# Attention and two gated MLPs on one core: the first MLP's weights are put together in another way, and head splitting begins one pair sooner

## The chip, the cores and the metric

The kernel runs on one core of a Trainium2 chip. The metric is the device time of one execution in microseconds (us), the median over the runs; lower is better. The engines are PE (TensorE, matrix products; PEld is its loading of weights), DVE (VectorE), ACT (ScalarE), POOL (GpSimd) and SP (SyncE, which issues the DMAs).

## The reference

Three stages, in float32. Attention has 4 batches, 8 heads, 576 positions and 64 columns a head; scores further than `tau` below the maximum of their row are cut off:

```
scores = scale * q @ k.T
scores = where(scores >= max(scores) - tau, scores, -1e9)
attn = exp(scores - max(scores)); attn = attn / (sum(attn) + 1e-9)
x = (attn @ v) gathered to 2304 tokens x 512
h = x @ w_in;  x = (h * sigmoid(h)) @ w_out        # first MLP, 512 -> 2048 -> 512
y = ((x @ w_a) * (x @ w_b)) @ w_out2               # second MLP, 512 -> 1536 -> 512
```

The weights are float64. The kernel reads each as two 32-bit words and builds the float32 value by hand.

## The kernel before, in words

**Products in two halves.** A float32 value is kept as a high half (rounded to the matmul's `fp32r` format) and a low half (the rest). A product is then three `fp32r` matmuls: weight low by data high, weight high by data high, weight high by data low.

**Attention.** The 4 x 8 heads are taken in 16 pairs, of which batch 0 has its four in two halves each. The unit of work is a tile of up to 128 query rows, numbered 0 to 143 (`softmax`): scores on PE (L537 or L544), the row minimum of the negated scores on DVE (L555), a threshold on DVE (L564), the exponential on ACT (L570), the mask on DVE (L573), then transposes on PE (L612), their copies out of PSUM on ACT, and the product with v on PE (L690). A head below tile `SPLIT_FROM` is loaded plainly (`load_head`) and its scores are float32 matmuls over 64 rows (L544). From there on it is split into halves first (`split_head`: cast on ACT, L457; subtraction on DVE, L460; five pieces on POOL, L463) and its scores are `fp32r` matmuls over 128 rows (L537).

**First MLP.** `w_in` and `w_out` are cut into 32 tiles of 128 x 512 (`w1_chunk`, `split_weight`). For each, a DMA brings the raw 64-bit words; ACT casts the low words to small integers (L358) and scales the high words (L363); DVE takes the sign bit (L369), shifts the scaled word left by three and joins the sign (L374); the low word is added, in four pieces on POOL for tiles 0 to 15, on DVE for 16 to 31 (L379); ACT casts the high half (L383), DVE subtracts the low half (L387). The tokens are taken in seven blocks, each against 16 slices of the hidden width: products up (L813), tanh, gate and halves (L823 to L832), products down (L873). These units follow one another strictly in order, so block 1 begins behind block 0, which needs all 32 weight tiles.

**Second MLP.** Its weights are prepared during attention and the first MLP and parked in DRAM; its products (L1184, L1270) come last.

**What sets the order.** `Plan` is a list scheduler that runs when the program is built: each task has an engine, a cost in ns, a rank and its dependencies; whenever an engine is free, its ready task of lowest rank goes next. The result is a fixed order for each engine. Ranks of attention are the tile's number plus `SHIFT`; the weight tile `i` has rank `W_AT + W_STEP * i + W_SHIFT[i]`; MLP work has ranks of 1000 and up, so it fills what attention leaves. `RINGS` gives the number of buffers: a task that takes a buffer waits, in order, until the one so many before it is freed. The raw weight tiles lie in a pool that is closed behind the last of the 32 (`closed0`), and the split heads' tiles are put in its place, so `split_head`'s cast is behind `closed0`.

Of the kernel before, what the change touches and what calls it, by code (L numbers as in the profile page):

```python
# [11 lines left out]

F32 = mybir.dt.float32
F32R = mybir.dt.float32r
U32 = mybir.dt.uint32
AF = mybir.ActivationFunctionType
ALU = mybir.AluOpType
PSUM = bass.MemoryType.PSUM
# [3 lines left out]
P = 128  # L22
# [23 lines left out]
N_YW, N_SW, N_TW = 14, 12, 6  # L46
# [5 lines left out]


W_AT, W_STEP = 2, 1.3
SHIFT = {1: -0.8, 8: 1.8, 14: 0.3, 19: -0.3, 23: -0.6, 25: -1.7, 27: -1.3, 28: -0.2, 29: 0.7,
         30: -0.4, 33: 0.9, 36: 1.0, 54: 1.9, 55: -2.5, 64: -2.1, 65: -1.1, 74: 5.6, 88: -1.0,
         96: -2.5, 108: -1.2, 115: -2.5, 129: 1.7, 132: -2.9}
W_SHIFT = {1: -1.8, 2: 3.2, 3: 3.9, 4: 6.8, 5: 3.5, 6: 3.4, 7: 5.1, 8: 4.1, 9: 7.4, 10: 7.9, 11:
           7.9, 12: 7.9, 13: 7.9, 14: 6.5, 15: 11.2, 16: 8.0, 17: 4.1, 18: 8.0, 19: 3.6, 20: 5.2,
           21: 6.3, 22: 10.2, 23: 10.2, 24: 8.2, 25: 8.5, 26: 11.1, 27: 10.2, 28: 10.2, 29: 10.2,  # L60
           30: -0.6, 31: 11.0}

SLACK = 2000

R_T, R_AV, R_EV, R_NORM = 2, 3, 1, -2
R_LD, R_SPLIT, R_AUX, R_MLP = -9, -6, -1, 1000

SPLIT_FROM = 54

EARLY = 16  # L70
IN_PSUM = 0
# [10 lines left out]
PIECE = 128  # L82

LO_ON = ("DVE",)

SCALE_ON = ("ACT",)
# [130 lines left out]
def dve_ns(n, fast=False):  # L217
    return int(n / (1.92 if fast else 0.96) + 67)


def pool_ns(n):
    return int(2.5 * n + 95)


def pieces(n, most):

    k = -(-n // most)
    return [slice(n * i // k, n * (i + 1) // k) for i in range(k)]
# [7 lines left out]
def fused_kernel(ctx: ExitStack, tc: tile.TileContext, qk, qk2, v, tau, w_in, w_out, w_a, w_b, w_o2, out):  # L236
# [9 lines left out]
    nc = tc.nc  # L246
    pl = Plan()
# [10 lines left out]
    def pool(stack, name, bufs, side="left", **kw):  # L258
        return stack.enter_context(tc.tile_pool(name=name, bufs=bufs, side=side, reuse_waits="tile", **kw))

    const = pool(ctx, "const", 1)
    pools = {n: pool(ctx, n, size) for n, size in (("wy", N_YW), ("ws", N_SW), ("wz", N_TW))}
    p1, p1x, px, att, attp, psb = (ExitStack() for _ in range(6))
    RINGS = dict(qk0=1, qk1=1, sp=2, aw=1, v=1, t=2, e=2, tl=1, si=1, pa=1, pb=1, sa=1, sb=1, tp=2, hb=1, hc=1, yc=1, yd=1, ye=1, yf=1, xr5=3, x5=5, g5=2, th5=1, av=1, x=1, xi=1, rs=1,
                 xr=2, xb=6, g=2, th=1, yo=2, wraw=2, wc=1, wt=2, wy=N_YW, ws=N_SW, wz=N_TW,
                 ur=2, uw=3, vr=1, vw=2, yr=1, pr=4, tm=4, a11=2, zh=3, zl=2, **{f"z{k}": 3 for k in range(5)})

    right = ctx.enter_context(ExitStack())
# [42 lines left out]
    scale = const.tile([P, 1], F32, name="scale")  # L311
# [14 lines left out]
    def on_pool(n, rank, fn, after, most):  # L326

        ts = []
        for o in pieces(n, most):
            ts.append(pl.add("Pool", pool_ns(o.stop - o.start), rank, lambda o=o: fn(o), after, behind=ts[-1:]))  # L330
        return ts

    def dma(rank, nbytes, fn, n=1, **kw):

        return pl.add("SP", 400 * n, rank, fn, nbytes=nbytes, **kw)


    def words(w):
        return w.bitcast(U32).rearrange("r (n two) -> r n two", two=2)

    w_in, w_out, w_a, w_b, w_o2 = (words(w) for w in (w_in, w_out, w_a, w_b, w_o2))
    wt, w_ready = {}, {}

    def split_weight(key, src, rank, dst, after=(), lo_engine="Pool", scale_engine="DVE", most=512, total_engine="Pool"):

        s = {}  # L350

        def load():
            s["raw"] = pools["wraw"].tile([P, 512, 2], U32, name="wraw")
            nc.sync.dma_start(out=s["raw"], in_=src)

        def low():
            s["t"] = pools["wtmp"].tile([P, 512], U32, name="wt", bufs=RINGS["wt"])
            nc.scalar.activation(out=s["t"], in_=s["raw"][:, :, 0], func=AF.Copy, scale=2.0**-29)  # L358

        def scale():  # L360
            s["c"] = pools["wtmp"].tile([P, 512], F32, name="wc")
            if scale_engine == "ACT":
                nc.scalar.activation(out=s["c"], in_=s["raw"][:, :, 1].bitcast(F32), func=AF.Copy, scale=2.0**-112)  # L363
            else:
                nc.vector.tensor_scalar(out=s["c"], in0=s["raw"][:, :, 1].bitcast(F32), scalar1=2.0**-112, scalar2=None,
                                        op0=ALU.mult)

        def sign():
            nc.vector.tensor_scalar(out=s["raw"][:, :, 1], in0=s["raw"][:, :, 1], scalar1=0x80000000, scalar2=None,  # L369
                                    op0=ALU.bitwise_and)  # L370

        def join():
            c = s["c"].bitcast(U32)
            nc.vector.scalar_tensor_tensor(out=c, in0=c, scalar=3, in1=s["raw"][:, :, 1],  # L374
                                           op0=ALU.logical_shift_left, op1=ALU.bitwise_or)

        def total(o):
            eng = nc.gpsimd if total_engine == "Pool" else nc.vector
            eng.tensor_tensor(out=s["t"][:, o], in0=s["c"][:, o].bitcast(U32), in1=s["t"][:, o], op=ALU.add)  # L379

        def hi():
            wt[key] = pools[dst].tile([P, 2, 512], F32R, name="w")
            nc.scalar.copy(out=wt[key][:, 0, :], in_=s["t"].bitcast(F32))  # L383

        def lo(o):
            eng = nc.gpsimd if lo_engine == "Pool" else nc.vector
            eng.tensor_tensor(out=wt[key][:, 1, o], in0=s["t"][:, o].bitcast(F32), in1=wt[key][:, 0, o].bitcast(F32),  # L387
                              op=ALU.subtract)

        a = dma(rank, P * 4096, load, take=["wraw"], behind=after)  # L390
        l = pl.add("ACT", 565, rank, low, [a], take=["wt"])
        c = pl.add(scale_engine, 565 if scale_engine == "ACT" else 335, rank, scale, [a], take=["wc"],
                   port=scale_engine == "DVE")
        h = pl.add("DVE", 335, rank, sign, [a, c], port=True)
        j = pl.add("DVE", dve_ns(512), rank, join, [h, c], port=True)
        if total_engine == "Pool":
            ts = on_pool(512, rank, total, [j, l], most)
        else:
            ts = [pl.add("DVE", dve_ns(512), rank, lambda: total(slice(0, 512)), [j, l], port=True)]
        pl.free("wc", ts[-1])  # L400
        pl.free("wraw", j, l)
        i = pl.add("ACT", act_ns(512), rank, hi, [ts[-1]], [dst], behind=after)
        if lo_engine == "Pool":
            os = on_pool(512, rank, lo, [i], most)
        else:
            os = [pl.add("DVE", dve_ns(512), rank, lambda: lo(slice(0, 512)), [i], port=True)]
        pl.free("wt", os[-1])
        w_ready[key] = (i, os[-1])
        return [a, l, c, h, j, *ts, i, *os]

    def w_pool(k):
        return "wy" if k < N_YW else "ws" if k < N_YW + N_SW else "wz"
# [1 line left out]
    def w1_chunk(i, rank):  # L414
        dst = w_pool(i)
        j, i = divmod(i, 8)
        engines = dict(scale_engine=SCALE_ON[i % len(SCALE_ON)], lo_engine=LO_ON[i % len(LO_ON)], most=PIECE, total_engine=("Pool", "DVE")[j > 1])
        if i < 4:
            return split_weight(("in", i, j), w_in[i * P:(i + 1) * P, j * 512:(j + 1) * 512], rank, dst, **engines)
        f = 4 * j + i - 4  # L420
        return split_weight(("out", f), w_out[f * P:(f + 1) * P, :], rank, dst, **engines)
# [93 lines left out]
    def at(n):  # L515
        return n + SHIFT.get(n, 0)

    def softmax(parts, total, slot, part):
# [47 lines left out]
        def exp():  # L566
            if early:
                nc.scalar.activation(out=s["e"], in_=s["s"][:, :, :NH], func=AF.Exp, scale=scale, bias=s["min"])
            else:
                nc.scalar.activation(out=s["e"], in_=s["t"], func=AF.Exp, scale=-1.0, bias=s["min"])  # L570

# [166 lines left out]
    def pair(b, c, halves):  # L738

        n = counter[0]  # L740
        if n < SPLIT_FROM:
            one, two = load_head(n, b, 2 * c, halves), load_head(n + 2, b, 2 * c + 1, halves)
# [53 lines left out]
    def mlp1_up(n, j, f):  # L796
# [21 lines left out]
        def tanh():  # L818
# [3 lines left out]
            s["gl"] = p.tile([P, tn], F32R, name="gl" + e, bufs=2)  # L822
            nc.scalar.activation(out=s["t"], in_=s["h"], func=AF.Tanh, scale=0.5)  # L823

# [26 lines left out]
    def mlp1_down(n, j, f):  # L851
# [33 lines left out]
        if f == NF - 1:  # L885
# [3 lines left out]
            def halve(k):  # L889
                def fn():  # L890
                    ys[j, k] = (yo_p if outs[k] == "yo" else pools["b5"]).tile([P, T2], F32, name=outs[k], bufs=RINGS[outs[k]])
                    if k % 2 == 0:
                        nc.scalar.activation(out=ys[j, k], in_=ys[j][k], func=AF.Copy, scale=0.5)
                    else:
# [28 lines left out]
    def split_unit(key, src, dst, rank, lane, behind):  # L923
# [4 lines left out]
        def load():  # L928
            if lane == "a":
                r = ap["qk"].tile([P, 2 * S], F32, name=raw)[:, :4 * 2 * P].bitcast(U32)  # L930
            else:
# [377 lines left out]


    w1 = [t for i in range(32) for t in w1_chunk(i, W_AT + W_STEP * i + W_SHIFT.get(i, 0))]

    def close_transit():
# [40 lines left out]
    for k in range(32):  # L1354
        j, i = divmod(k, 8)
# [15 lines left out]
    def close_spare():  # L1371
# [8 lines left out]
                     behind=[up_last[0], down_last[0], closed_x, closed_b, *stored.values(), *(t for *_, t in y_dma)])  # L1380
    for u in range(NT // UNIT):
        y = load_y(u, pe_at[0])
        for g in range(NG):
            p = mlp2_up(u, g, y)
# [47 lines left out]
```

## Time and profile before

| | |
|---|---|
| median of 3 runs | 1111.31 us (1109.4 to 1111.57) |
| profiled execution | 1110.28 us, span 1108.5 us |
| PE busy | 1085.0 us, 98% of the span |
| DVE busy | 835.2 us, 75% |
| ACT busy | 589.2 us, 53% |
| POOL busy | 171.4 us, 15% |
| granted TensorE clock | 0.998 of full speed |

The table is an average over stages: attention with the first MLP as filling (to about 490 us), the rest of the first MLP (to about 710 us), the second MLP. A row of the profile's groups has the line, engine and operation, output and inputs, shapes and count, then busy time and mean duration of one, then the engine's idle time before it and what ended that. Lines are those of the kernel before.

### The profile page before, as it was taken

The page shows a single profiled execution, that of the slowest core. Times are in us where ns is not written, and L with a number is a line of the kernel's source. Part 1 is how long each engine was busy: PE and PEld are TensorE (multiplying, and loading weights), DVE is VectorE, ACT ScalarE, POOL GpSimd, SP SyncE. Part 2 cuts the span into 40 slices and gives each one's busy share as a digit, 9 for nine tenths or more (in the row PEclk, how much of TensorE's full clock was granted, in tenths as well). Part 3 has the DMA queues.
Part 4 walks back from the last instruction along what each step waited for, and adds up shares of the span by engine and source line. Part 5 has one row for each costly group of instructions (what it writes and reads, how often), then busy time and mean ns, then how long its engine had stood idle before and what let it go on. Part 6 is the DMA issues. An engine that isn't in the chain of part 4 may idle for free.

```text
span 1108.5 us, 19427 instructions
## 1 busy us (share of the span) xinstructions
PE 1085.0 (98%) x6986; PEld 967.7 (87%) x6986; DVE 835.2 (75%) x1723; ACT 589.2 (53%) x1108; POOL 171.4 (15%) x311
## 2 busy tenths in 40 slices
PE   8899889999999999999999999999999999999998
PEld 5567667988888889899888888899999999999998
DVE  8998998898898998848989863266874668536664
ACT  7888888677778777855665642211341114401132
POOL 3455103333432433321000000000000000000000
PEclk9999999999999999999999999999999999999999
DMA  6655544444444553247998726488889888888882
GB/s 198 193 168 179 185 155 142 143 135 146 137 146 141 165 165 113 91 130 235 301 287 271 256 81 227 148 248 255 259 305 307 250 257 248 285 283 251 251 254 80
DMA packets 115952, 223.59 MB, mean 202 GB/s; under 512 B 9088, under 2 KB 76304, under 8 KB 115856
## 3 DMA queue, kind: packets, MB, share of 16 engines
q1 hardware_dynamic: 115712, 222.34, 63.4%
q8 instruction: 56, 0.92, 0.3%
q14 instruction: 40, 0.33, 0.1%
q10 hardware_dynamic: 144, 0.00, 0.0%
HBM read 175.05 MB, written 47.26 MB: 201 GB/s over the span
## 4 chain that ended last, share of the span: by engine, by line
PE 58%; DMA 1%; DVE 0%; ACT 0%; issue 0%; DVEq 0%; POOL 0%; SPq 0%
PE pr L1184 24%; PE pr L1270 11%; PE hb L813 6%; PE hc L813 5%; PE sb L873 3%; PE yd L873 2%; PE yc L873 2%; PE yf L873 2%; PE ye L873 2%; DMA yr<-yT_d 1%; PE av L690 1%; PE sa L537 0%; PE tp L612 0%; DVE zl L1035 0%; DVE t L555 0%
## 5 line engine op out<-in xcount | busy, mean ns | idle before, releaser
L1184 PE MATMUL pr<-w 128*128 128x384 f32 x1512 | 262.6, 334 | 0.0
L1184 PEld LDWEIGHTS pr<-w 128*128 128x128 f32 x1512 | 262.2, 188 | 0.1
L813 PE MATMUL hb<-xh,w 128*128 128x256 f32 (+1 forms) x704 | 156.2, 313 | 3.1 <-DVE th L826 2.2
L573 DVE SCALAR_TENSOR_TENSOR e<-t,thr,e 128x576 f32<-128x576 f32 x144 | 124.0, 864 | 15.9 <-ACT e L570 14.1
L1270 PE MATMUL pr<-zh,w 128*128 128x384 f32 x504 | 128.3, 336 | 0.0
L813 PEld LDWEIGHTS hb<-xh,w 128*128 128x128 f32 x704 | 113.4, 190 | 16.4 <-DVE th L826 5.0
L570 ACT ACTIVATE e<-t,min 128x576 f32<-128x576 f32 x144 | 111.4, 776 | 26.1 <-DVE t L555 24.6
L555 DVE TENSOR_SCALAR_CACHE_REDUCE t<-sa,nscale 128x576 f32<-128x576 f32 x136 | 110.1, 810 | 14.8 <-PE sa L537 12.1
L813 PE MATMUL hb<-xl,w 128*128 128x256 f32 (+1 forms) x352 | 106.9, 304 | 0.0
L873 PE MATMUL sb<-gh,w 128*128 128x256 f32 (+1 forms) x576 | 96.6, 300 | 0.0
L612 PE MATMUL tp<-ident,e 128*128 128x128 f32 x576 | 88.3, 278 | 4.7 <-DVE e L573 4.1
L1270 PEld LDWEIGHTS pr<-zh,w 128*128 128x128 f32 x504 | 91.1, 188 | 0.0
L612 PEld LDWEIGHTS tp<-ident,e 128*128 128x128 f32 x576 | 64.8, 141 | 23.3 <-issue 11.2
L1270 PE MATMUL pr<-zl,w 128*128 128x384 f32 x252 | 84.8, 336 | 0.2 <-DVE zl L1035 0.2
L873 PEld LDWEIGHTS sb<-gh,w 128*128 128x128 f32 x576 | 79.7, 190 | 5.0 <-DVE w L387 1.0
L463 POOL TENSOR_TENSOR sp<-qk,sp 64x115 fp32r<-64x115 f32 (+1 forms) x100 | 60.7, 641 | 113.4 <-ACT sp L457 69.3
L1196 ACT COPY yo<-pr 128x384 f32<-128x384 f32 x18 | 8.6, 480 | 123.7 <-PE pr L1184 123.7
L537 PE MATMUL sa<-sp 128*128 128x288 f32 (+1 forms) x400 | 70.6, 302 | 0.2 <-DVE t L555 0.2
L832 DVE TENSOR_TENSOR gl<-th,gh 128x256 fp32r<-128x256 f32 (+1 forms) x112 | 61.2, 546 | 12.4 <-ACT gh L829 12.0
L1031 ACT CAST zh<-z 128x768 fp32r<-128x768 f32 x45 | 37.6, 836 | 61.6 <-PE pr L1270 39.2
L813 PEld LDWEIGHTS hb<-xl,w 128*128 128x128 f32 x352 | 66.9, 190 | 2.8
L829 ACT CAST gh<-th 128x256 fp32r<-128x256 f32 (+1 forms) x112 | 52.0, 464 | 28.5 <-DVE th L826 28.2
(155 smaller groups left out, 1987.4 us busy)
## 6 DMA issues: line engine op xcount, KB each, us to landing
w<-wab_d SPq DMA_DIRECT2D x126, 512.0 KB
w<-wo_d SPq DMA_DIRECT2D x63, 512.0 KB
qk<-qk SPq DMA_DIRECT2D x20, 608.0 KB
wab_d<-aw SPq DMA_DIRECT2D x11, 896.0 KB
wab_d<-uw SPq DMA_DIRECT2D x11, 896.0 KB
wraw<-w_in SPq DMA_DIRECT2D x16, 512.0 KB
wraw<-w_out SPq DMA_DIRECT2D x16, 512.0 KB
wo_d<-uw SPq DMA_DIRECT2D x9, 896.0 KB
```

The lines of the kernel that those rows point to most:

```text
L463: nc.gpsimd.tensor_tensor(out=s["t"][D:, o], in0=s["r"][D:, o], in1=s["t"][D:, o].bitcast(F32), op=ALU.subtract)
L537: nc.tensor.matmul(s["s"][:r + m, j, :NH], lhsT=hd["t"][:, c - r:c + m], rhs=hd["t"][:, o:o + NH], start=(k == 1), stop=(k == 2), skip_gro ...
L555: nc.vector.tensor_scalar(out=s["t"], in0=s["s"][:, :, :NH], scalar1=nscale, scalar2=None, op0=ALU.mult, op1=ALU.min, accum_out=s["min"])
L570: nc.scalar.activation(out=s["e"], in_=s["t"], func=AF.Exp, scale=-1.0, bias=s["min"])
L573: nc.vector.scalar_tensor_tensor(out=s["e"], in0=s["s"][:, :, :NH] if early else s["t"], scalar=s["thr"], in1=s["e"], op0=ALU.is_ge if ear ...
L612: nc.tensor.transpose(tp[:, k * P:(k + 1) * P], slot["e"][:, o:o + P], ident)
L813: nc.tensor.matmul(s["h"], lhsT=w[:, a, o:o + P], rhs=xx, start=(c == 0 and k == 0), stop=(c == NC - 1 and k == 2))
L829: nc.scalar.copy(out=s["gh"], in_=s["t"])
L832: nc.vector.tensor_sub(out=s["gl"], in0=s["t"], in1=s["gh"].bitcast(F32))
L873: nc.tensor.matmul(ys[j][e // per][:, e % per * tn:(e % per + 1) * tn], lhsT=w[:, a, e * P:(e + 1) * P], rhs=gs[j, f][g], start=(f == 0 an ...
L1184: nc.tensor.matmul(bank[:, m, :TN], lhsT=w["w"][:, 2 * m + k, a], rhs=y[i][x][:, k, :TN], start=(i in (1, 6, 5) and k == 0 and q == 0), st ...
L1270: nc.tensor.matmul(bank[:, c, :TN], lhsT=w["w"][:, 2 * e + c, a], rhs=z[x][:, e], start=(i in (1, 6, 5) and sl == 0 and e == 0 and q == 0) ...
```

## The change

The word that DVE shifts no longer gets its sign at the shift. The low words (as small integers) and the sign words are written side by side into one tile `x` of 1026 words, low words in 0 to 511, sign words in 512 to 1023. The shift is a plain one of the scaled word in place. Then one custom DVE instruction adds 1024 16-bit halves: the first operand and the output are the shifted words, halves in their natural order; the second operand takes for each word the low half of its low word and the high half of its sign word, which lie 1025 halves apart. The adds on POOL are gone. The rings become: raw tiles 3 (from 2), scaled words 2 (from 1), side-by-side tile 1 (in place of two tiles of low words). `SPLIT_FROM` goes from 54 to 45, so tiles 45 to 53 use split heads. The tables `SHIFT` and `W_SHIFT` get other values, `SHIFT` many more.

```diff
-SPLIT_FROM = 54
+SPLIT_FROM = 45
...
-                 xr=2, xb=6, g=2, th=1, yo=2, wraw=2, wc=1, wt=2, wy=N_YW, ws=N_SW, wz=N_TW,
+                 xr=2, xb=6, g=2, th=1, yo=2, wraw=3, wc=2, wx=1,  wy=N_YW, ws=N_SW, wz=N_TW,
...
         def low():
-            s["t"] = pools["wtmp"].tile([P, 512], U32, name="wt", bufs=RINGS["wt"])
-            nc.scalar.activation(out=s["t"], in_=s["raw"][:, :, 0], func=AF.Copy, scale=2.0**-29)
+            s["x"] = pools["wtmp"].tile([P, 1026], U32, name="wx", bufs=RINGS["wx"])
+            nc.scalar.activation(out=s["x"][:, :512], in_=s["raw"][:, :, 0], func=AF.Copy, scale=2.0**-29)
...
         def sign():
-            nc.vector.tensor_scalar(out=s["raw"][:, :, 1], in0=s["raw"][:, :, 1], scalar1=0x80000000, scalar2=None,
+            nc.vector.tensor_scalar(out=s["x"][:, 512:1024], in0=s["raw"][:, :, 1], scalar1=0x80000000, scalar2=None,
                                     op0=ALU.bitwise_and)
 
-        def join():
+        def shift():
             c = s["c"].bitcast(U32)
-            nc.vector.scalar_tensor_tensor(out=c, in0=c, scalar=3, in1=s["raw"][:, :, 1],
-                                           op0=ALU.logical_shift_left, op1=ALU.bitwise_or)
-
-        def total(o):
-            eng = nc.gpsimd if total_engine == "Pool" else nc.vector
-            eng.tensor_tensor(out=s["t"][:, o], in0=s["c"][:, o].bitcast(U32), in1=s["t"][:, o], op=ALU.add)
+            nc.vector.tensor_scalar(out=c, in0=c, scalar1=3, scalar2=None, op0=ALU.logical_shift_left)
+
+        def total():
+            c = s["c"].bitcast(U16).rearrange("p (n two) -> p n two", two=2)
+            limbs = s["x"].bitcast(U16)[:, :2050].rearrange("p (two n) -> p two n", two=2)[:, :, :1024:2]
+            nc.vector._custom_dve(ADD32_U16LIMBS, out=c, in0=c, in1=limbs.rearrange("p two n -> p n two"))
...
-        l = pl.add("ACT", 565, rank, low, [a], take=["wt"])
-        c = pl.add(scale_engine, 565 if scale_engine == "ACT" else 335, rank, scale, [a], take=["wc"],
-                   port=scale_engine == "DVE")
-        h = pl.add("DVE", 335, rank, sign, [a, c], port=True)
-        j = pl.add("DVE", dve_ns(512), rank, join, [h, c], port=True)
-        if total_engine == "Pool":
-            ts = on_pool(512, rank, total, [j, l], most)
-        else:
-            ts = [pl.add("DVE", dve_ns(512), rank, lambda: total(slice(0, 512)), [j, l], port=True)]
-        pl.free("wc", ts[-1])
-        pl.free("wraw", j, l)
+        c = pl.add(scale_engine, 565 if scale_engine == "ACT" else 335, rank, scale, [a], take=["wc"], port=scale_engine == "DVE")
+        j = pl.add("DVE", 335, rank, shift, [c], port=True)
+        l = pl.add("ACT", 565, rank, low, [a], take=["wx"])
+        h = pl.add("DVE", 335, rank, sign, [a], port=True, behind=[l])
+        ts = [pl.add("DVE", dve_ns(512), rank, total, [h, j, l], port=True)]
+        pl.free("wraw", c, l, h)
+        pl.free("wx", ts[-1])
```

`dve_ns(512)` is 600 ns, the planner's figure for the add as before. High and low half are taken from the scaled word's tile, which now holds the whole value and is freed behind the low half.

## Rows read from the trace of the kernel before

**Rows 1.** The page, part 1: busy time, share of the span, instructions.
```profile
PE 1085.0 (98%) x6986; PEld 967.7 (87%) x6986; DVE 835.2 (75%) x1723; ACT 589.2 (53%) x1108; POOL 171.4 (15%) x311
```

**Rows 2.** Windows: length, busy time (instructions) of PE, PEld, DVE, ACT, POOL; clock, DMA.
```profile
5.00:186.00 181.00, 163.75 (x1159) 113.32 (x1159) 169.20 (x439) 153.50 (x320) 60.07 (x107) 0.99 0.58 178
192.00:475.00 283.00, 281.94 (x2268) 252.82 (x2267) 249.86 (x671) 218.55 (x453) 93.52 (x161) 1.00 0.44 139
```

**Rows 3.** Waits to 190 us: engine, line, whom it awaited; total us, times, longest.
```profile
PEld sa L544 <- DVE t L555: 11.2, 22, 1.4
...
DVE e L573 <- ACT e L570: 5.4, 10, 1.2
```

**Rows 4.** Timeline of DVE, 143 to 148 us: start, duration, what.
```profile
143.19 0.42 DVE L369 TENSOR_SCALAR wraw<-wraw 128x512 uint32<-128x512 uint32 x1
143.53 0.81 DVE L555 TENSOR_SCALAR_CACHE_REDUCE t<-sa,nscale 128x576 f32<-128x576 f32 x1
...
144.60 0.69 DVE L374 SCALAR_TENSOR_TENSOR wc<-wc,wraw 128x512 uint32<-128x512 uint32 x1
145.21 0.21 DVE L564 TENSOR_SCALAR thr<-min,tadd 128x1 f32<-128x1 f32 x1
145.33 0.68 DVE L379 CUSTOM_DVE_ANT_0 wt<-wc,wt 128x1024 uint16<-128x1024 uint16 x1
145.93 0.81 DVE L573 SCALAR_TENSOR_TENSOR e<-t,thr,e 128x576 f32<-128x576 f32 x1
...
146.67 0.81 DVE L555 TENSOR_SCALAR_CACHE_REDUCE t<-sa,nscale 128x576 f32<-128x576 f32 x1
...
147.41 0.69 DVE L387 TENSOR_TENSOR w<-wt,w 128x512 fp32r<-128x512 f32 x1
```

**Rows 5.** Timeline of DVE at the end of the weights.
```profile
186.58 0.69 DVE L387 TENSOR_TENSOR w<-wt,w 128x512 fp32r<-128x512 f32 x1
```

**Rows 6.** Groups by line: busy us, mean ns of one, idle time before.
```profile
L379 POOL TENSOR_TENSOR wt<-wc,wt 128x128 uint32<-128x128 uint32 x64 | 34.6, 569 | 45.3 <-DVE wc L374 25.3 <-DVE thr L564 8.4 <-DVE sum L495 5.3
...
L387 DVE TENSOR_TENSOR w<-wt,w 128x512 fp32r<-128x512 f32 x32 | 22.4, 703 | 0.9 <-ACT w L383 0.7
...
L970 DVE TENSOR_TENSOR uw<-uw 128x896 fp32r<-128x896 f32 x20 | 21.8, 1090 | 4.6 <-ACT uw L967 4.1
...
L379 DVE CUSTOM_DVE_ANT_0 wt<-wc,wt 128x1024 uint16<-128x1024 uint16 x16 | 11.0, 684 | 0.0
```

**Rows 7.** Timeline of PE, around 145 us and from 194 to 198 us.
```profile
144.61 0.76 PE L544 MATMUL sa<-qk 64*128 64x288 f32 x4
145.29 0.51 PE L813 MATMUL hb<-xh,w 128*128 128x256 f32 x2
...
194.58 0.69 PE L537 MATMUL sa<-sp 128*128 128x288 f32 x4
195.11 0.40 PE L813 MATMUL hb<-xh,w 128*128 128x256 f32 x2
...
196.18 1.12 PE L873 MATMUL sb<-gh,w 128*128 128x256 f32 x8
197.14 0.65 PE L873 MATMUL sb<-gl,w 128*128 128x256 f32 x4
```

**Rows 8.** Windows of lines L813, L873 (PE, PEld) and L555 (DVE), in this order.
```profile
225.00:475.00 250.00, 71.51 (x462) 60.81 (x460) 1.00 0.43 137
...
225.00:475.00 250.00, 68.90 (x456) 59.99 (x456) 1.00 0.43 137
...
225.00:475.00 250.00, 65.79 (x161) 1.00 0.43 137
```

**Rows 9.** Masks at 12 to 118 and 122 to 186 us: minimum, median, maximum ns.
```profile
L573 DVE SCALAR_TENSOR_TENSOR e<-t,thr,e x36: 780/883/1125, 12.3 to 115.3; 128x576 f32<-128x576 f32 x36
...
L573 DVE SCALAR_TENSOR_TENSOR e<-t,thr,e x15: 775/812/1018, 123.1 to 183.0; 128x576 f32<-128x576 f32 x15
```

**Rows 10.** Waits to 190 us, of ACT for the single buffer wc.
```profile
ACT wc L363 <- DVE wt L379: 1.5, 2, 0.8
```

More of the change, by code (lines that the diff above doesn't have):

```diff
@@ L9 @@
 from concourse import mybir
+from concourse.dve_ops import ADD32_U16LIMBS
 from concourse._compat import with_exitstack
@@ L15 @@
 U32 = mybir.dt.uint32
+U16 = mybir.dt.uint16
 AF = mybir.ActivationFunctionType
@@ L54 @@
 W_AT, W_STEP = 2, 1.3
[L55 to L61, printed above, removed]
+SHIFT = {0: -16.6, 1: -5.0, 2: -0.5, 3: 0.7, 4: 2.3, 5: 0.3, 7: -5.9, 8: -15.6, 9: 2.6, 11:
[10 rows of a table added]
+W_SHIFT = {0: -9.1, 1: -3.6, 2: 3.4, 3: 34.4, 4: 0.4, 5: 14.0, 6: 5.9, 7: 4.9, 8: 18.1, 9: 0.7,
[3 rows of a table added]
 SLACK = 2000
@@ L342, in fused_kernel, with split_weight @@
     wt, w_ready = {}, {}
-    def split_weight(key, src, rank, dst, after=(), lo_engine="Pool", scale_engine="DVE", most=512, total_engine="Pool"):
+    def split_weight(key, src, rank, dst, after=(), lo_engine="Pool", scale_engine="DVE", most=512):
         s = {}
@@ L356, in low @@
         def low():
-            s["t"] = pools["wtmp"].tile([P, 512], U32, name="wt", bufs=RINGS["wt"])
-            nc.scalar.activation(out=s["t"], in_=s["raw"][:, :, 0], func=AF.Copy, scale=2.0**-29)
+            s["x"] = pools["wtmp"].tile([P, 1026], U32, name="wx", bufs=RINGS["wx"])
+            nc.scalar.activation(out=s["x"][:, :512], in_=s["raw"][:, :, 0], func=AF.Copy, scale=2.0**-29)
         def scale():
-            s["c"] = pools["wtmp"].tile([P, 512], F32, name="wc")
+            s["c"] = pools["wtmp"].tile([P, 512], F32, name="wc", bufs=RINGS["wc"])
             if scale_engine == "ACT":
@@ L381, in hi @@
         def hi():
             wt[key] = pools[dst].tile([P, 2, 512], F32R, name="w")
-            nc.scalar.copy(out=wt[key][:, 0, :], in_=s["t"].bitcast(F32))
+            nc.scalar.copy(out=wt[key][:, 0, :], in_=s["c"])
         def lo(o):
             eng = nc.gpsimd if lo_engine == "Pool" else nc.vector
-            eng.tensor_tensor(out=wt[key][:, 1, o], in0=s["t"][:, o].bitcast(F32), in1=wt[key][:, 0, o].bitcast(F32),
+            eng.tensor_tensor(out=wt[key][:, 1, o], in0=s["c"][:, o], in1=wt[key][:, 0, o].bitcast(F32),
@@ L406, in split_weight @@
             os = [pl.add("DVE", dve_ns(512), rank, lambda: lo(slice(0, 512)), [i], port=True)]
-        pl.free("wt", os[-1])
+        pl.free("wc", os[-1])
         w_ready[key] = (i, os[-1])
-        return [a, l, c, h, j, *ts, i, *os]
+        return [a, c, h, j, l, *ts, i, *os]
     def w_pool(k):
@@ L416, in w1_chunk @@
         j, i = divmod(i, 8)
-        engines = dict(scale_engine=SCALE_ON[i % len(SCALE_ON)], lo_engine=LO_ON[i % len(LO_ON)], most=PIECE, total_engine=("Pool", "DVE")[j > 1])
+        engines = dict(scale_engine=SCALE_ON[i % len(SCALE_ON)], lo_engine=LO_ON[i % len(LO_ON)], most=PIECE)
         if i < 4:
```

13 rows, old and new, of tables (SHIFT, W_SHIFT) are left out of this document.

## The prediction

> **What bounds the kernel now.** I read the busy table first [rows 1]: PE is busy for 98% of the span, so little seems left. The windows say where the rest is [rows 2]. From 192 us on PE has no gap worth naming: 281.94 of 283.00 us up to 475. From 5 to 186 us it lacks 17 us even by its records, and the records flatter it, since a lone matmul keeps it "busy" for its whole latency: 1159 matmuls in 181 us are 6.4 a microsecond there, against 2268 in 283, or 8.0, afterwards. In that first stretch DVE is the full engine, 169.20 of 181.00 us. The view of waits agrees: PE's score matmuls wait for DVE's row minimum (L555), while DVE's own longest wait comes to 5.4 us [rows 3]. DVE's timeline shows it packed end to end [rows 4].
>
> Why the stretch ends near 187 us: the last weight of the first MLP is finished by DVE at 186.58 + 0.69 us [rows 5], and the split heads may only begin behind it. Until then PE has attention and token block 0 of the first MLP for filling and nothing else, because the units of that MLP follow one another in order and block 0 needs all 32 weight tiles. Afterwards it has more filling than it can do, to the end of the kernel. So the end time is PE's work plus PE's idle time before the last weight tile, and that idle time is set by how much DVE must do until then.
>
> **The weight tile's cost on DVE.** What counts is start to start, read from the timeline [rows 4]: sign (L369) 143.19 to 143.53, 0.34 us; join (L374) 144.60 to 145.21, 0.61; the 16-bit add (L379) 145.33 to 145.93, 0.60. The low half (L387) has a record of the add's length (0.69 and 0.68): 0.60. Before, tiles 0 to 15 have their add on POOL and cost DVE 0.34 + 0.61 + 0.60 = 1.55 us; tiles 16 to 31 cost 2.15. After, all 32 cost shift + sign + add + low half. The shift has sign's form (one input, 32-bit words, SBUF): 0.34. The add is the open one.
>
> Its cost T has two ends. Below: it stays the instruction of today, 1024 halves in 684 ns [rows 6], 0.60 start to start. Above: one half per tick. The f32 subtractions give the tick: 512 elements 703 ns, 896 elements 1090 ns [rows 6], 387/384 = 1.008 ns an element. Then 1024 halves take 703 + 512 x 1.008 = 1219 ns, 535 more than today, T = 1.135. Today's 684 ns for 1024 halves is under a tick for each, so two go at a time, and in today's operands the two halves of a word are neighbours. In the new second operand they lie 1025 halves apart. No row shows that, so both ends stay; I take the upper, since what the row's pace rests on, a word's halves side by side in every operand, is gone.
>
> [...] No row shows a step of 1025.
>
> Sum over tiles, T = 1.135: each costs 0.34 + 0.34 + 1.135 + 0.60 = 2.42 us; 16 x (2.42 - 1.55) + 16 x (2.42 - 2.15) = 13.9 + 4.3 = **+18.2 us of DVE**, all ahead of the last weight tile. With T = 0.60: 1.88 a tile, 16 x 0.33 - 16 x 0.27 = +1.0 us.
>
> **One pair of heads moved behind the weights.** Nine tiles of scores (45 to 53) now come after them. One tile costs DVE 0.74 (L555, 146.67 to 147.41) + 0.74 (L573, 145.93 to 146.67) + 0.12 (threshold, 145.21 to 145.33) = 1.60 us [rows 4], nine 14.4: the last weight is due that much sooner. But PE has their work still to do. In the full stretch 225 to 475 us, 462 + 456 MLP matmuls at 0.12 us (8 from 196.18 to 197.14 [rows 7]) take 110.2; the other 139.8 us serve 161/2 = 80.5 tiles (two records a tile) [rows 8], 1.74 each, nine 15.7. Net +1.3 us. The trade of tiles against weights is thus nearly nothing, and the new order among them moves little.
>
> On PE a split score part takes 0.53 (194.58 to 195.11), an unsplit one 0.68 (144.61 to 145.29) [rows 7]: ten parts in the pair, -1.5 us. The two heads' splitting (a cast on ACT, a 640-element subtraction on DVE, five pieces on POOL each) and their two larger loads fall behind the weights, where DVE is busy 249.86 and ACT 218.55 of 283 us [rows 2]: covered. Without that cover the two subtractions, between the 512- and 896-element rows [rows 6], would cost about 1.7 us.
>
> **What softens it.** POOL loses 64 adds of 569 ns [rows 6]. It is not on the path; its gain is in the mask, which took 883 ns by the median while POOL did those adds and 812 after [rows 9]: 36 x 0.071 = 2.6 us at most, I take 2. DVE idles 181.00 - 169.20 = 11.8 us in the stretch; a DVE that is behind finds its inputs ready. None or all of it may be used; I take 5, near the 5.4 us that DVE waits for ACT's exponentials [rows 3], which would be done in time.
>
> **Rings and waits.** A third raw tile lets loads lead; ACT, which reads them, idles 27.5 us in the stretch [rows 2], so I count no gain. The new side-by-side tile has one buffer: the next tile's cast (ACT) and sign (DVE) wait for this tile's add. Queued behind that cast on ACT are exponentials and PSUM copies, for which mask and transposes wait. The nearest row is today's single buffer wc, whose next writer on ACT waits 1.5 us in all for the add [rows 10]. I cost it at nothing; its upper end is 32 x 0.535 = 17, if every lengthening came back once more through ACT, and I keep 3 of that for the range, twice the row. The order is written for an add of 0.6, so a longer one shifts the engines' queues alike; the longer rank tables I cost at nothing, with DVE's 11.8 us as the bound below.
>
> **Sum.** 18.2 + 1.3 - 1.5 - 2 - 5 = +11.0 us on the profiled execution's 1110.28 us (span 1108.5 and 1.8 around it): 1121.3. The median of the runs is 1111.31, one above that execution; I predict **1121 us**. Its own range: nothing absorbed and 3 for the ring, 19.5 - 1.5 + 3 = +21.0, 1131; all idle time and 2.6 us used, 19.5 - 1.5 - 2.6 - 11.8 = +3.6, 1114.
>
> **Rivals.**
> - The add keeps its pace (T = 0.60). Then 1.0 + 1.3 - 1.5 - 2.6 = -1.8, and up to 5 of idle time: 1103.5 to 1108.5, 1106 the middle, faster. For it: the same operation on as many halves. Against: the second operand's halves are apart. The place is the add in each of the 32 tiles; 11.0/32 = 0.34 us, so it decides from an add of about 1219 - 340 = 880 ns downward. Chance 0.12.
> - The new ranks use DVE's idle time in full and close small gaps of PE later. The records show only 1 us of gap from 192 to 475, but of the 1.74 us per tile the scores need 0.53 x 10/9 = 0.59; the other 1.15 are transposes, value products, and gaps hidden under latencies. If 0.1 of it is gap, 90 tiles hold 9 us. That gives 3.6 - 9 = -5 at best, 1105, and 1110 in the middle. Against: DVE's waits are latencies of one chain. Chance 0.18 (0.08 faster, 0.07 within the bound, 0.03 slower).
> - DVE's lateness multiplies in the queues, through the single side-by-side tile and ACT: above 1131. For it, the order was computed with 0.6; against, the single wc buffer costs 1.5 us today. Chance 0.08.
> - The forecast: 0.62.
>
> A measurement of this kernel can tell 0.2%, 2.2 us. Faster: 0.12 + 0.08 = 0.20; within: 0.07; slower: 0.03 + 0.08 + 0.62 = 0.73. The range goes from 1104 (the add at its pace, with some idle time used) to 1131; the forecast's own is 1114 to 1131.
>
> **What the new profile would show.** The add at 1.2 us x32 on DVE, the shift at 0.42, no weight adds on POOL; the last low half near 187 + 18 - 14 - 7 = 184 us with 45 tiles of scores ahead of it, and fewer matmuls started by then; after it PE full, as now. An add near 0.68 us proves the first rival. The last weight well before 175 us with an add of 1.2 us would mean that the order did more than I allow; a PE with gaps after it, that something else than DVE's load bounds the kernel. If the add is slow and the time still falls, the step that ties PE's idle time to DVE's load is wrong.

## The result, and the profile after

The changed kernel takes 1118.47 us (median of 4 runs, 1117.93 to 1119.48) against 1111.28 us before. The ratio is 1.0069, interval 1.0052 to 1.0087: slower by 0.7%, or 7.2 us. The forecast was 1121 us, its own range 1114 to 1131.

The first thing to look up is the open one, the add. These are the groups of DVE from 5 to 174 us of the changed kernel (busy us, mean ns of one, idle time before; L389 the add, L379 the sign, L384 the shift, L397 the low half, L579 the mask):

```profile
L389 DVE CUSTOM_DVE_ANT_1 wc<-wc,wx 128x1024 uint16<-128x1024 uint16 x32 | 39.8, 1245 | 0.4
L579 DVE SCALAR_TENSOR_TENSOR e<-t,thr,e 128x576 f32<-128x576 f32 x45 | 37.2, 832 | 2.3 <-PE tp L624 1.5 <-ACT e L576 0.7
...
L397 DVE TENSOR_TENSOR w<-wc,w 128x512 fp32r<-128x512 f32 x31 | 21.7, 703 | 0.2 <-ACT w L393 0.2
L379 DVE TENSOR_SCALAR wx<-wraw 128x512 uint32<-128x512 uint32 x32 | 14.3, 445 | 0.0
L384 DVE TENSOR_SCALAR wc<-wc 128x512 uint32<-128x512 uint32 x32 | 13.6, 426 | 0.3 <-ACT wc L373 0.3
```

The add takes 1245 ns where it took 684 [rows 6]. The records of the 32 weight tiles sum to 39.8 + 22.5 + 14.3 + 13.6 = 90.2 us (22.5 is the low half with its 32nd tile, from the groups to 200 us), against 13.7 + 22.3 + 11.0 + 22.4 = 69.4 before (L369, L374, L379 on DVE, L387).

The windows show the same two stretches as before [rows 2], with the few microseconds between them (columns as there):

```profile
5.00:174.00 169.00, 147.15 (x982) 98.19 (x981) 165.28 (x403) 138.98 (x285) 24.08 (x36) 0.95 0.59 182
174.00:181.00 7.00, 5.86 (x49) 5.66 (x49) 4.17 (x8) 3.88 (x10) 5.09 (x11) 1.00 0.13 42
181.00:475.00 294.00, 293.58 (x2340) 258.83 (x2339) 260.18 (x701) 230.51 (x477) 105.08 (x175) 1.00 0.44 140
```

DVE idles 169.00 - 165.28 = 3.7 us ahead of the last weight tile, against 11.8 before. PE starts 982/169 = 5.8 matmuls a microsecond, fewer than the 6.4 before; from 181 us on it is as full as ever. DVE's wait for the exponentials, 5.4 us before [rows 3], has nearly gone:

```profile
DVE e L579 <- PE tp L624: 1.5, 1, 1.5
DVE e L579 <- ACT e L576: 0.7, 2, 0.5
```

DVE's timeline at the end of the weights, to be held against [rows 4, 5]:

```profile
171.01 0.42 DVE L384 TENSOR_SCALAR wc<-wc 128x512 uint32<-128x512 uint32 x1
171.35 0.41 DVE L832 SCALAR_TENSOR_TENSOR th<-th,hb 128x256 f32<-128x256 f32 x1
171.68 0.42 DVE L379 TENSOR_SCALAR wx<-wraw 128x512 uint32<-128x512 uint32 x1
172.23 1.27 DVE L389 CUSTOM_DVE_ANT_1 wc<-wc,wx 128x1024 uint16<-128x1024 uint16 x1
173.42 0.64 DVE L838 TENSOR_TENSOR gl<-th,gh 128x256 fp32r<-128x256 f32 x1
173.98 1.72 DVE L397 TENSOR_TENSOR w<-wc,w 128x512 fp32r<-128x512 f32 x2
```

Shift to next start 0.34 us, add to next start 1.19, and the last low half is done at 175.7 us: 11.6 us sooner than the 187.3 before, with 45 tiles of scores ahead of it instead of 54. A further number is needed below: the time at which block 0 of the first MLP is through, taken as the start of the 385th matmul of that MLP (a block has 384). It was 188.2 us before and is 180.5 now. Block 0 thus ends 7.7 us sooner and the kernel 8.0 us later (span 1116.5 against 1108.5).

### The profile page after: what moved, and what is told of

Its sections match the earlier page's. It is cut to its first block, busy times and chain, and to the rows that moved or that the text cites. A ratio compares the mean times of both kernels' runs of the same rounds, so it can differ in the third digit from the quotient of the medians.

```text
span 1116.5 us, 19330 instructions
## 1 busy us (share of the span) xinstructions
PE 1088.1 (97%) x6956; PEld 966.9 (87%) x6956; DVE 849.5 (76%) x1741; ACT 592.7 (53%) x1110; POOL 149.1 (13%) x257
## 4 chain that ended last, share of the span: by engine, by line
PE 85%; DVE 9%; issue 2%; DMA 2%; ACT 1%; SPq 0%; DVEq 0%; ACTq 0%
PE pr L1190 23%; PE pr L1276 12%; PE hb L819 11%; PE sb L879 8%; PE av L696 6%; PE sa L543 5%; PE hc L819 5%; PE tp L618 4%; PE yc L879 2%; PE yd L879 2%; PE yf L879 2%; PE ye L879 2%; DVE e L579 2%; DVE wc L389 2%; DVE t L561 2%
## 5 line engine op out<-in xcount | busy, mean ns | idle before, releaser
L579 DVE SCALAR_TENSOR_TENSOR e<-t,thr,e 128x576 f32<-128x576 f32 x144 | 121.8, 849 | 11.6 <-ACT e L576 8.7
L819 PEld LDWEIGHTS hb<-xh,w 128*128 128x128 f32 x704 | 113.3, 190 | 14.6 <-DVE th L832 3.5
L469 POOL TENSOR_TENSOR sp<-qk,sp 64x115 fp32r<-64x115 f32 (+1 forms) x110 | 66.4, 637 | 115.6 <-ACT sp L463 74.9
L543 PE MATMUL sa<-sp 128*128 128x288 f32 (+1 forms) x440 | 77.9, 303 | 0.0
L725 POOL TENSOR_TENSOR x<-x,xi 128x128 f32<-128x128 f32 (+2 forms) x80 | 48.5, 630 | 186.3 <-DMA xi<-r_d 119.7
L838 DVE TENSOR_TENSOR gl<-th,gh 128x256 fp32r<-128x256 f32 (+1 forms) x112 | 59.3, 530 | 11.0 <-ACT gh L835 10.6
```

The costliest lines, as they stand in the source:

```text
L469: nc.gpsimd.tensor_tensor(out=s["t"][D:, o], in0=s["r"][D:, o], in1=s["t"][D:, o].bitcast(F32), op=ALU.subtract)
L543: nc.tensor.matmul(s["s"][:r + m, j, :NH], lhsT=hd["t"][:, c - r:c + m], rhs=hd["t"][:, o:o + NH], start=(k == 1), stop=(k == 2), skip_gro ...
L579: nc.vector.scalar_tensor_tensor(out=s["e"], in0=s["s"][:, :, :NH] if early else s["t"], scalar=s["thr"], in1=s["e"], op0=ALU.is_ge if ear ...
L819: nc.tensor.matmul(s["h"], lhsT=w[:, a, o:o + P], rhs=xx, start=(c == 0 and k == 0), stop=(c == NC - 1 and k == 2))
L838: nc.vector.tensor_sub(out=s["gl"], in0=s["t"], in1=s["gh"].bitcast(F32))
```

## The experiments

The theory (A): DVE's load sets when block 0 of the first MLP is through, PE idles until then, and afterwards it is full, so the end follows block 0's end one for one, plus the work of the attention tiles that are still to do. The rivals: the new ranks and the split pair lose the time (B), the add is slow for another reason than its operand (C). All ratios are against runs of the kernel before on the same chip (its median there was 1110.1 to 1111.3 us), so differences of a few microseconds between two runs are read from the ratios. "Tiles before the last weight" counts the tiles masked by DVE until the last low half is done; "block 0 through" and the span are of the profiled execution.

| run | median us | ratio (interval) | tiles before the last weight | block 0 through | span | span less block 0 |
|---|---|---|---|---|---|---|
| before | 1111.3 | 1 | 54 | 188.2 | 1108.5 | 920.3 |
| changed | 1118.5 | 1.0069 (1.0052 to 1.0087) | 45 | 180.5 | 1116.5 | 936.0 |
| e1 | 1102.7 | 0.9934 (0.9919 to 0.9949) | 45 | 165.8 | 1101.3 | 935.5 |
| e2 | 1117.1 | 1.0062 (1.0040 to 1.0084) | 52 | 193.9 | 1115.9 | 922.0 |
| e3 | 1136.2 | 1.0231 (1.0216 to 1.0246) | 45 | 189.9 | 1134.2 | 944.3 |
| e4 | 1103.4 | 0.9946 (0.9926 to 0.9966) | 45 | 166.3 | 1101.6 | 935.3 |
| e5 | 1105.5 | 0.9963 (0.9952 to 0.9974) | 52 | 180.7 | 1102.7 | 922.0 |
| e6 | 1130.3 | 1.0186 (1.0171 to 1.0201) | 45 | 179.1 | 1128.0 | 948.9 |
| e7 | 1123.3 | 1.0118 (1.0103 to 1.0133) | 48 | 191.9 | 1121.7 | 929.8 |
| e8 | 1120.8 | 1.0085 (1.0072 to 1.0098) | 45 | 171.9 | 1117.4 | 945.5 |
| e9 | 1118.5 | 1.0082 (1.0065 to 1.0099) | 45 | 180.4 | 1115.2 | 934.8 |
| e10 | 1119.2 | 1.0071 (1.0058 to 1.0084) | 54 | 192.7 | 1115.8 | 923.1 |
| e11 | 1117.1 | 1.0055 (1.0040 to 1.0069) | 54 | 194.8 | 1115.0 | 920.2 |
| e12 | 1104.4 | 0.9944 (0.9930 to 0.9958) | 45 | 168.1 | 1102.8 | 934.7 |

**e1, the add's operand alone.**
```diff
-            limbs = s["x"].bitcast(U16)[:, :2050].rearrange("p (two n) -> p two n", two=2)[:, :, :1024:2]
-            nc.vector._custom_dve(ADD32_U16LIMBS, out=c, in0=c, in1=limbs.rearrange("p two n -> p n two"))
+            limbs = s["x"].bitcast(U16)[:, :1024].rearrange("p (n two) -> p n two", two=2)
+            nc.vector._custom_dve(ADD32_U16LIMBS, out=c, in0=c, in1=limbs)
```


> The changed kernel with one thing different: the add's second operand is read as 1024 halves in a row (the first 512 words of the side-by-side tile), so the sign words are left out of the result; every instruction, rank and buffer stays. Theory A (the slow add loads DVE, and PE idles until block 0 of the first MLP is through): the add falls from 1.24 to about 0.68 us, 32 x 0.56 = 18 us less DVE ahead of the last weight tile; DVE's idle time there grows back from 4 to about 10 us, so the time falls by 9 to 14 us, to 1104 to 1110 us. Theory B (the new ranks and the pair of heads moved cost the time, the add is hidden): 1116 to 1120 us. Theory C (the add is slow for another reason than its operand's halves lying apart): add still near 1.24 us, time unchanged.

The group of the add in e1:
```profile
L389 DVE CUSTOM_DVE_ANT_0 wc<-wc,wx 128x1024 uint16<-128x1024 uint16 x32 | 21.9, 685 | 0.2
```
The same 1024 halves take 685 ns once they are neighbours. B and C fall; the order of the work on DVE, ACT and POOL is that of the changed kernel. The time goes 15 us below the changed kernel (0.9934 against 1.0069), a little more than A said, because less idle time came back (7.9 us up to the last weight against 3.7, not 10): block 0 is through 14.7 us sooner.

**e11, the mirror in the kernel before: one cost doubled.** The adds of tiles 16 to 31 read a tile of zeros in halves 512 apart.
```diff
-            eng.tensor_tensor(out=s["t"][:, o], in0=s["c"][:, o].bitcast(U32), in1=s["t"][:, o], op=ALU.add)
...
+            t, c = (s[k].bitcast(U16).rearrange("p (n two) -> p n two", two=2) for k in "tc")
+            apart = zeros.bitcast(U16).rearrange("p (two n) -> p n two", two=2)
+            nc.vector._custom_dve(ADD32_U16LIMBS, out=t, in0=c, in1=apart)
```


> The kernel before with one cost doubled: the adds of tiles 16 to 31 on DVE take as second operand halves that lie 512 apart, in a tile of zeros (so the low words of these tiles are left out of the result); order and all else the same. Theory A (one half per tick, and DVE's load ahead of the last weight tile sets the time): add 1.22 to 1.25 us, 16 x 0.56 = 9 us more of DVE where it idles little, 1115 to 1120 us. Theory C (distance of the halves does not matter): add 0.69 us and the time within 2 us of before.

```profile
L388 DVE CUSTOM_DVE_ANT_1 wt<-wc,zeros 128x1024 uint16<-128x1024 uint16 x16 | 19.7, 1232 | 0.0
```
1232 ns at a distance of 512, 1245 at 1025 in the changed kernel, 685 in e1 as neighbours: 13 ns between the two distances, 547 and 560 from them to neighbours. 16 x 0.548 = 8.8 us of DVE put block 0 back by 6.6 us and the span by 6.5. TensorE's clock has no part in that: ahead of 175 us it was at half for 3.4 us, as in the kernel before.

**e2 and e3, the two parts of the change by themselves.** e2 is the new assembly with its rings and the old `SHIFT`, `W_SHIFT` and `SPLIT_FROM = 54`; e3 is the old assembly and rings with the new tables and 45.

> The new weight assembly and its rings alone, with the ranks and SPLIT_FROM = 54 of the kernel before. Theory A: DVE gets 19 us more in the first stretch, of which its idle time takes up to 8 and the quicker masks some 4, so 1115 to 1120 us, the last weight tile near 194 us. Theory B (ranks and split pair are the loss): 1109 to 1113 us.

> The new ranks and SPLIT_FROM = 45 alone, with the weight assembly and rings of the kernel before. Theory A: DVE's load before the last weight tile falls by nine tiles (14 to 16 us), PE has nine tiles more to do after it: the two cancel within 3 us, 1107 to 1113 us, last weight tile near 172 us. Theory B: 1116 to 1120 us.

e2's time came as A said: the assembly alone costs what the whole change costs (1.0062 against 1.0069). Its last weight was done at 189.7 us, not near 194. e3 is a miss of 23 us for A as I had put it, though not for B's reason either: the whole change has the same tables and takes 18 us less. Ahead of the last weight DVE now waits (total, times, longest):
```profile
DVE e L581 <- ACT e L578: 11.4, 15, 4.5
DVE wraw L377 <- ACT wc L371: 6.0, 7, 1.9
DVE w L395 <- ACT w L391: 4.0, 6, 1.1
```
So the new tables do not suit the old assembly. e6 asks whether the rings are why:
```diff
-... wraw=2, wc=1, wt=2, ...
+... wraw=3, wc=2, wt=2, ...
...
-            s["c"] = pools["wtmp"].tile([P, 512], F32, name="wc")
+            s["c"] = pools["wtmp"].tile([P, 512], F32, name="wc", bufs=RINGS["wc"])
```


> The ranks-and-split-only kernel (weight assembly of before) with larger rings: 3 raw tiles, 2 scaled words, 2 low words. Theory R (the new ranks lost 25 us there because one scaled-word buffer and two raw tiles chained the weight tiles one behind the other): DVE's idle time ahead of the last weight tile falls from 25 us to under 14 and the time to 1104 to 1115 us. Theory P (it was the add in four pieces on POOL behind its own queue): still above 1125 us.

Half of it: block 0 is through at 179.1 us instead of 189.9, and DVE's idle time falls from 25.4 to 14.6 us, yet the kernel still takes 1130. R's time is missed. P's time came, but its reason is not shown: part of the loss moved to after block 0 (last column of the table, 948.9 against 935). Where that part lies is seen best in e8.

**e4, e5 and e12, the whole value with neighbouring halves.**
```diff
-            s["x"] = pools["wtmp"].tile([P, 1026], U32, name="wx", bufs=RINGS["wx"])
-            nc.scalar.activation(out=s["x"][:, :512], in_=s["raw"][:, :, 0], func=AF.Copy, scale=2.0**-29)
+            s["x"] = pools["wtmp"].tile([P, 512, 2], U16, name="wx", bufs=RINGS["wx"])
+            nc.scalar.activation(out=s["x"][:, :, 0], in_=s["raw"][:, :, 0], func=AF.Copy, scale=2.0**-29)
...
-            nc.vector.tensor_scalar(out=s["x"][:, 512:1024], in0=s["raw"][:, :, 1], scalar1=0x80000000, scalar2=None,
+            nc.vector.tensor_scalar(out=s["x"][:, :, 1], in0=s["raw"].bitcast(U16)[:, :, 3], scalar1=0x8000, scalar2=None,
...
+            nc.vector._custom_dve(ADD32_U16LIMBS, out=c, in0=c, in1=s["x"])
```


> The whole value again, but the side-by-side tile is laid out as 16-bit halves in the order of the words: ACT writes the low word's integer as a 16-bit half to every even place, DVE writes the masked top half of the high word to every odd place, and the add reads 1024 halves in a row. All else as in the changed kernel. Theory A: add 0.68 us, sign near 0.42 us (0.69 if a 16-bit operand with a step costs the double pace), so 1104 to 1110 us (up to 1113 with the slow sign). Theory B: 1116 to 1120 us.

> The interleaved assembly with its quick add and the new rings, but the ranks and SPLIT_FROM = 54 of the kernel before. Theory A (DVE's load before block 0 of the first MLP is through sets the time, the order matters little): against the weights-only run it loses 18 us of DVE and gets some idle time back, 1101 to 1107 us, as the interleaved run. Theory B (the new order gave the interleaved run its gain): 1109 to 1112 us.

> The interleaved kernel once more, with more rounds, for its interval against the kernel before: 1101 to 1106 us by every theory, below both kernels.

The groups of e12 from 5 to 165 us:
```profile
L388 DVE CUSTOM_DVE_ANT_0 wc<-wc,wx 128x1024 uint16<-128x1024 uint16 x32 | 22.0, 686 | 0.7 <-ACT wx L368 0.2
L379 DVE TENSOR_SCALAR wx<-wraw 128x512 uint16<-128x512 uint16 x32 | 15.2, 474 | 0.0
```
The quick add with the full value: 0.9944 (0.9930 to 0.9958), the best version with the full value, below both kernels; e4 came out a little under A's range. e5, with the old order, gains nearly as much. So a quick add is worth 1.2% or 14 us in the new order (e4 against the changed kernel) and 1.0% or 11 us in the old one (e5 against e2), while the order, with the pair that goes with it, moves 1 to 2 us either way, which is within the intervals.

**e7, the pair moved back**, is the changed kernel with `SPLIT_FROM = 54`.

> The changed kernel with SPLIT_FROM = 54, all else as changed. Theory A: moving nine tiles ahead of or behind the weights is a trade of about equal parts (DVE 16 us against PE 15.7 less 1.5): 1116 to 1123 us. Theory B (the earlier splitting is what costs): 1108 to 1113 us.

At the upper edge of A: 1123.3, some 5 us above the changed kernel. With the new tables only 48 tiles, not 54, come ahead of the last weight, so this moves three tiles and not nine. The last column bears out PE's side of the trade: with 48 tiles it is 929.8, between 920.3 (54) and 936.0 (45). DVE's side it does not: at 1.6 us a tile block 0 would be 5 us later than in the changed kernel, and it is 11.4 later (the last weight 7.2, at 182.9). Why is open.

**e8, a second side-by-side tile** (`wx=2`) in e4.

> The interleaved kernel with two side-by-side tiles in place of one. Theory A (DVE's load sets the time, the single tile costs next to nothing): within 3 us of the interleaved kernel, 1100 to 1106 us. Theory Q (the single tile chains ACT and DVE): ACT's wait for the add goes and 4 us or more with it, under 1099 us.

A miss by every theory: one more buffer, and 16 us slower than e12. The planner, which knows of the buffer, wrote another order with ranks found without it: ACT's work differs from e4's from its tenth instruction on. So e8 does not test the single tile by itself. Against e12 block 0 is through 3.8 us later, and 10.8 us more come after it. PE's windows of e8, then of e4:
```profile
460.00:480.00 20.00, 18.96 (x143) 15.55 (x141) 15.09 (x44) 13.87 (x30) 8.70 (x18) 1.00 0.30 99
480.00:500.00 20.00, 17.72 (x128) 13.96 (x129) 9.40 (x28) 10.58 (x24) 2.04 (x5) 1.00 0.09 22
```
```profile
460.00:480.00 20.00, 20.00 (x164) 17.25 (x163) 12.14 (x38) 12.84 (x32) 3.35 (x6) 1.00 0.05 17
480.00:500.00 20.00, 20.00 (x169) 20.00 (x169) 10.19 (x21) 10.55 (x24) 9.01 (x19) 1.00 0.65 199
```
In e4 PE is full there; in e8 it starts 143 and 128 matmuls in 20 us instead of 164 and 169. By 475 us e4 has masked all 144 tiles, e8 only 137, with 1548 matmuls of the first MLP done against 1532: the order let attention fall behind, and its last tiles run with little beside them. e3 and e6 show the same lag, counted from the end of block 0: the last mask starts 319.7 us after it in e8, 318.1 in e3 and 322.7 in e6, against 307.4 to 308.6 in the five other runs with 45 tiles. Why these orders space attention so is open; it was not tried with ranks made for them.

**e9, more filling on PE.**
```diff
-                for _ in range(min(16, int(FILL * t["task"]["gap"] / 109))):
+                for _ in range(min(16, int(1.2 * t["task"]["gap"] / 109))):
```


> The changed kernel with twice as many filling transposes in PE's gaps (the order and all else the same). Theory A: the stretches at half clock ahead of 175 us (17 us in the changed kernel, 3.4 before) get shorter, but DVE sets the pace there, so the time moves by less than 3 us from 1118.5. Theory K (the half clock costs a good part of the 7 us): 1111 to 1115 us.

The first window of the changed kernel and of e9 (the column behind POOL is the granted clock):
```profile
0.00:25.00 25.00, 20.01 (x103) 12.37 (x103) 20.49 (x63) 16.41 (x31) 1.72 (x11) 0.80 0.58 194
```
```profile
0.00:25.00 25.00, 19.09 (x106) 11.98 (x106) 20.57 (x63) 16.48 (x31) 1.70 (x11) 0.86 0.59 194
```
With 67 filling transposes instead of 30 the stretches at half clock ahead of 175 us came to 13.7 us instead of 17.1, and the ratio did not move beyond its interval. DVE's busy time in the window is the same. That speaks for A, but as the half clock only shrank by a fifth, what all of it costs is not settled by this run. e11 helps: there DVE's load alone cost 6.5 us, with no more half clock than before.

**e10, POOL's adds in the kernel before put on DVE** (`total_engine="DVE"` for all tiles).

> The kernel before with the adds of tiles 0 to 15 on DVE too (quick ones, 0.69 us), so that POOL adds no weights. Theory A: DVE gets 16 x 0.60 = 9.6 us more, the masks to 118 us fall from 883 to about 814 ns (36 x 0.07 = 2.5 us), idle time takes some: 1109 to 1115 us. Theory P (POOL's adds slow nothing): masks stay near 880 ns and the time is 1114 to 1120 us.

Masks from 12 to 118 us (minimum, median, maximum ns), to be held against the first of [rows 9]:
```profile
L573 DVE SCALAR_TENSOR_TENSOR e<-t,thr,e x33: 789/814/1016, 12.4 to 116.1; 128x576 f32<-128x576 f32 x33
```
A's reason is borne out, and P's falls: without POOL's adds the mask goes from 883 to 814 ns. A's time was 4 us too low, and the measured one lies in P's range: DVE gave up only 1 of its 12 us of idle time, block 0 is through 4.5 us later, and 2.8 us more come after block 0, which I can't place.

## Why the prediction was right, step by step

- **The add goes at one half per tick.** Worked out 1219 ns, measured 1245; the lower end, 684, is what e1 gives when the halves are neighbours, and e11 shows the slow pace at another distance. The means of the add of these weights over the runs: 684 to 690 ns with neighbours in every operand (the kernel before, e1, e3, e4, e8, e10, e12); 1232 with halves 512 apart in one operand alone (e11); 1245 and 1262 with halves 1025 apart in it (the changed kernel, e2).
- **DVE gets 18.2 us more for the weights.** The records grew by 90.2 - 69.4 = 20.8 us; 16 more instructions overlap their neighbours by 0.08 each, so about 19.5 us start to start.
- **The end hangs on block 0 and on the tiles left.** This is the step that the runs bear out best. In the last column of the table the time after block 0 is 920.2 to 923.1 us in the three runs with 54 tiles ahead of the weights, 922.0 in the two with 52, 929.8 with 48, and 934.7 to 936.0 in five with 45. Nine tiles moved cost 936.0 - 920.3 = 15.7 us after block 0, where I had 15.7 - 1.5 = 14.2; the saving by split scores does not show. That moving tiles is a trade of about equal parts shows from e5 to e4: seven tiles fewer ahead of the weights, block 0 14.4 us sooner, 13.3 more after it. Three runs lie off this line (e3, e6, e8, 9 to 14 us above it). In each the new tables met rings or an assembly that they were not made with; but e2 and e5, where the old tables met new rings and a new assembly, lie on it, so that alone does not explain it.
- **The mis-sized term is what softens the load.** I put the last weight at 184 us, 18.2 - 14.4 - 2 - 5 = 3.2 us sooner than before, and block 0 with it. The last weight came 11.6 us sooner. If each moment from 5 us to the last weight is given to the DVE record that started last, the two traces split this as follows: weights +19.1 (I had 18.2), row minima, thresholds and masks -19.5 (I had 14.4 and 2 for the quicker masks), idle time -8.2 (I had 5), gates -1.9 and the rest -1.0 (I had nothing). The masks' median fell as I took it (883 to 814, 31 masks, 2.1 us; e10 shows the cause); a tile's three operations took 97.6/54 = 1.81 us of DVE before, not the 1.60 that I read from one. Block 0 gained only 7.7 of the 11.6: it ended 4.8 us behind the last weight, 0.9 before. Two gate units fewer were done by the last weight (14 L838 against 16 L832), and these ran behind it with little beside them: from 174 to 181 us DVE is busy for 4.17 of 7. So block 0 was 4.5 us sooner than forecast and the rest 1.5 longer (15.7 - 7.7 = +8.0 on the span, against 14.2 - 3.2 = +11.0). That the two errors have opposite signs, and that units left behind took back 3.9 us which the sum did not have, is luck; the terms were not each as close as the total.
- **The new order is worth little: right here, and no rule.** With the rings that the tables go with, the order moves about 1 us up (changed against e2) or 2 us down (e4, e12 against e5), and the intervals of these pairs overlap. With other rings or the old assembly the same tables lose 16 us and more (e8, e3, e6).
- **The rivals.** An add that keeps its pace: it doesn't, and the price I gave it, 1106, was too high; e1 and e4 are at 1103. Ranks that use up the idle time: it is used up (3.7 us left), but e2 with the old ranks has 4.1. e5, which is e2 with the quick add, has 7.2, and the kernel before 12.0 when counted to the last weight. So it is the new assembly with its rings (12.0 to 7.2) and the longer add (7.2 to 4.1), not the ranks. Lateness that multiplies through the single tile: ACT's wait for the add in the waits of the changed kernel (total, times, longest) is

```profile
ACT wx L368 <- DVE wc L389: 4.5, 10, 0.7
```

That is three times the old wc wait [rows 10]. Ahead of the last weight it can have cost DVE no more than the 3.7 us that DVE idles there, of which 2.2 are the two waits for other work shown above. No run takes the single tile away and leaves the order as it is.

## What to carry to other kernels

The 16-bit add of these weights took 684 to 690 ns for 1024 halves that were neighbours in both operands, and 1232 to 1262 when one of its two operands had its halves 512 or 1025 apart; so write the producers such that the halves lie as neighbours, even if a producer gets a step (here +0.03 us on the sign and +0.11 on ACT's cast against -0.56 on the add). It is no rule for every 16-bit instruction: the sign of e12, with one operand, reads at a step of 4 and writes at one of 2, and its 512 elements took 474 ns, 0.93 each, less than the tick of 1.008 from the f32 rows. Where one engine paces the work up to a gate and another is full behind it, add up the pacing engine's start-to-start times ahead of the gate and the other engine's work left behind it; in eleven of the fourteen kernels here the end follows the two. An order found for one set of buffers need not be one for another: one buffer more, with the order that the planner then wrote, cost 16 us, though the old ranks in the new rings (e2, e5) lost nothing of the kind. So ranks have to be tried again with each such change.

## What the runs showed of the hardware that was not expected

- Three of the 32 adds of the changed kernel stand right behind the sign whose words they read. Two of them start 0.13 us behind its end (sign 171.68 + 0.42, add 172.23; sign 169.27 + 0.42, add 169.82), the third 0.04 (sign 91.92 + 0.41, add 92.37). The sign at 171.68, which reads nothing of the gate before it, starts 0.08 us ahead of the gate's end (171.35 + 0.41), a difference of 0.21 us. In e1 the add does not read what the sign wrote, and in the same place it starts 0.09 us ahead of the sign's end (158.13 + 0.42, add 158.46). Another instruction between the two would gain little here, as there are only these three.
- Operands of 16 bits with a step: the sign's mean went from 445 ns in the changed kernel to 474 in e4 and e12, and ACT's cast of the low words, whose output went to 16 bits and got a step of 2 at once, took 790 ns by the median in e4 against 677 in the changed kernel:

```profile
L368 ACT ACTIVATE wx<-wraw x32: 761/790/828, 8.7 to 157.5; 128x512 uint16<-128x512 uint32 x32
```
- TensorE's granted clock fell to 0.50 of full speed early in the changed kernel (from 11 to 21 us), 0.80 over the first 25 us, where PE started 103 matmuls; before it was 1.00 with 125. It fell with the quick add too: e1 has 0.86 there with 102 matmuls, and e5, with 105, the changed kernel's 0.80, though e5 is 6 us faster than the kernel before by its span.
